# First input block of a gated state-space/GELU kernel: two 128-column pieces loaded apart, and the second one's transposes moved between matmuls

## The chip, the cores and the metric

The kernel runs on one core of a Trainium2 chip. The metric is the device time of one execution in microseconds. It is given as the median over several executions; 9 were timed for the kernel before. One further execution was recorded by the hardware profiler, and all profile numbers come from that one.

## The reference, cut to what matters

`x` has 2048 rows (time steps) of D = 640 numbers in bf16. A gate mixes a diagonal state-space layer with a dense GELU layer:

```python
g = sigmoid((x * gate_w).sum(-1, keepdims=True))
# a: h_t = Lam_bar * h_{t-1} + x_t @ B_bar^T   (complex diagonal recurrence, P = 640)
#    a = 2 * Re(h @ C^T) + x * Dskip
# b: gelu(x @ w1 + b1) @ w2 + b2               (F = 1728)
out = g * a + (1 - g) * b
```

The change concerns only the very first part of this: the product of the first 512 rows of `x` with the first 1024 columns of `w1`.

## The kernel before, in words

The 2048 rows are taken in four blocks of 512 (`q` = 0 to 3). TensorE (PE) contracts over partitions, so it needs `x` transposed: `xT[q]` holds, for each of five groups `k` of 128 input columns, a 128 x 512 tile. Most of the `xT` tiles come from transposing DMAs. Two of them, `k` = 0 and 1 of the first block, are made differently: `x` is loaded as it lies into `xn[0]` (the load `xna`, L370, 512 rows of 256 numbers, 256 KB), PE transposes it in 128 x 128 pieces against an identity matrix (L422 to L433, `xt0` to `xt3`, two pieces each, into PSUM banks 7, 6, 5 and 4), and VectorE (DVE) copies each pair from PSUM into `xT[0]` as bf16 (L436, `xc0` to `xc3`).

Before these transposes stands `warm` (L413): seven matmuls of a constant, whose result is not used. After them comes `m1_first` (L634): the first eight of the 128-column groups `jf` of `w1`, one PSUM bank (0 to 7) each, with `k` in the outer loop, so that the 40 matmuls need the tiles of `w1` and `xT[0]` one `k` after the other. Below, (k, jf) names one of them. For `k` = 0 and `jf` = 0 and 1 they are cut in halves of 256 columns, so that the first needs only `xc0`. Bank 7 serves first a transpose, then `cols` (L449: the transpose of the packed small vectors `rows`, which gives the biases and the recurrence's constants), and only then (0, 7) and (1, 7).

All further work (rest of the first product L665, `B` projection L708, second product L932, `C` projection L981, the last block's output L795 and L844) follows on PE in an order that does not change. DVE does the recurrence (L748) and the elementwise work, ScalarE (ACT) GELU and evictions.

The order is made by a small list scheduler (`Sched.order`, L43). Each operation names the keys that it reads and writes, an engine, an estimated duration and a priority; the scheduler runs an estimate of time and, on each engine, takes the released operation of lowest priority number. The result is a fixed instruction order per engine; waits are semaphores that `Emitter.wait` (L116) sets where a key was made on another engine. A DMA is an operation of the queue that issues it: `sp` (SyncE's queue, most loads, one after the other), `pool` (GpSimd's queue), and in the changed kernel also `act`. The head of SP's queue before is: `xna`; `w1` for `k` = 0; `w1` for `k` = 1; transposing load of `xT` for `k` = 2; `w1` for 2; `xT` for 3; `w1` for 3 in two parts; `xT` for 4; `w1` for 4; and then the rest of `w1`, the `B` matrices and everything else. The five loads into `rows` (L390 to L394) are on POOL's queue; the last of them is `b1b`.

Of the kernel before, what the change touches and what calls it, by code (L numbers as in the profile page):

```python
# [147 lines left out]
class Prog:  # L148
# [8 lines left out]
    def op(self, name, eng, dur, reads, writes, fn, prio=None, lat=0.0, after=()):  # L157
        deps = {}
        for k in reads:
            for w in self.last_w.get(k, ()):  # L160
                deps[w.idx] = w
        for k in writes:
            for w in self.last_w.get(k, ()):
                deps[w.idx] = w
            for r in self.last_r.get(k, ()):
                deps[r.idx] = r
        for a in after:
            deps[a.idx] = a
        deps = list(deps.values())
        E = self.E  # L170

        def run(eg, deps=deps, eng=eng, fn=fn):
            E.wait(eng, *[d.done for d in deps if not (eng == "pe" and d.eng == "pe")])
            return fn()

        it = self.sch.add(name, eng, dur, deps, run, prio=prio, lat=lat)
        for k in writes:
            self.last_w[k] = [it]
            self.last_r[k] = []
        for k in reads:  # L180
            self.last_r.setdefault(k, []).append(it)
        return it


def bass_gated_mix__ssm_conv_s5__dense_activation_gelu__prompt_kernel(
# [18 lines left out]
    _, S, D = A_x.shape  # L204
    P = A_Lambda_re.shape[0]
    F = B_w1.shape[1]
# [8 lines left out]
    FL = F - (NF - 1) * 128  # L215
# [6 lines left out]
    x2 = A_x[0]  # L222
# [3 lines left out]
    with ExitStack() as es:  # L226

        def SB(name, shape, dt):
            return es.enter_context(nc.sbuf_tensor(name, list(shape), dt))

        xT = [SB(f"xT_{i}", [128, KD, 512], BF16) for i in range(NQ)]
        xn = [SB(f"xn_{i}", [128, 4, D], BF16) for i in range(2)]
# [9 lines left out]
        rows = SB("rows", [128, 128], BF16)  # L242
# [11 lines left out]
        ident = SB("ident", [128, 128], BF16)  # L254
# [40 lines left out]
        PS = [es.enter_context(nc.psum_tensor(f"ps{i}", [128, 512], FP32)) for i in range(8)]  # L295
# [13 lines left out]
        op = pr.op  # L309

        def inc(eng, ins):
            return E.inc(eng, ins, eng + "_s")

        def dma_inc(eng, ins, sem):
            SEM(sem)
            E.count.setdefault(sem, 0)
            ins.then_inc(sems[sem], 16)
            E.count[sem] += 16
            return (sem, E.count[sem])

        def d_act(n):
            return 0.26 + n * 0.00084
# [4 lines left out]
        def d_mm(n):  # L327
            return n / 2400.0 + 0.004


        def load(name, eng, sem, dst, src, writes, prio, dur=0.5, lat=2.5, reads=(), after=()):
            def fn():
                with nc.allow_non_contiguous_dma(reason="columns of small vectors"):
                    return dma_inc(eng, engines[eng].dma_start(dst, src), sem)
            return op(name, eng, dur, reads, writes, fn, prio=prio, lat=lat, after=after)
# [16 lines left out]
        nmain = (NF - 1) * 128  # L352
# [7 lines left out]
        def w1load(k, eng, prio):  # L360
            edges = [0] + ([WSPLIT[k] * 128] if k in WSPLIT else []) + [FW]
            for i, (f0, f1) in enumerate(zip(edges, edges[1:])):
                load(f"w1_{k}{i}", eng, f"l_w1{k}{i}", W1sb[:, k, f0:f1], B_w1[k * 128:(k + 1) * 128, f0:f1], [("w1", k, i)], prio=prio + 0.1 * i, lat=2.6)

        def w1tok(k, jf):
            return ("w1", k, int(jf >= WSPLIT.get(k, NW)))

        KN = 2

        load("xna", "sp", "l_xna", xn[0][:, :, 0:KN * 128], x2[0:512, 0:KN * 128].rearrange("(c p) d -> p c d", p=128), ["xna"], 0, dur=0.45, lat=2.0)  # L370
        w1load(0, "sp", 1)
        w1load(1, "sp", 1.3)
        xtrans(0, range(KN, KN + 1), 1.6, 0.8)
# [10 lines left out]
        RT = 3 * KP + NF - 1  # L384
# [5 lines left out]
        for i, (nm, (r0, src)) in enumerate(ROWS.items()):  # L390
            src = src.rearrange("(k p) -> k p", p=128)
            load(nm, "pool", "l_" + nm, rows[r0:r0 + src.shape[0], :], src, [nm], prio=-50 + i, dur=0.6)
        load("b1b", "pool", "l_b1b", rows[RT:RT + 1, :].rearrange("o (a p) -> o a p", a=2),
             B_b1[nmain:F].rearrange("(o p) -> o p", o=1).unsqueeze(1).broadcast_to([1, 2, FL]), ["b1b"], prio=-45, dur=0.6)  # L394

        def f_iota():
            inc("pool", nc.gpsimd.iota(io_i[:, :], pattern=[[1, 128]], base=0, channel_multiplier=-1))
# [13 lines left out]
        one = nc.const_aps.tensor(1.0, [128, 1], BF16)  # L411

        def f_warm():  # L413
            t = None
            for n in (512,) * 6 + (256,):
                t = nc.tensor.matmul(PS[4][:, 0:n], one.broadcast_to([128, 128]), one.broadcast_to([128, n]), start=True, stop=True)
            return inc("pe", t)

        op("tload", "act", 1.5, (), ["tl"], lambda: inc("act", nc.scalar.activation(tl[:, :], one, ACT.Exp)), prio=-1000)
        op("warm", "pe", 2.7, (), [("bank", 4)], f_warm, prio=-1000)  # L420

        for i, (k, c0, c1) in enumerate(((0, 0, 2), (0, 2, 4), (1, 0, 2), (1, 2, 4))):  # L422
            bank = (7, 6, 5, 4)[i]
            pt = PS[bank][:, 0:(c1 - c0) * 128]

            def f_xt(k=k, pt=pt, c0=c0, c1=c1):
                t = None
                for c in range(c0, c1):
                    t = nc.tensor.matmul(pt[:, (c - c0) * 128:(c - c0 + 1) * 128], xn[0][:, c, k * 128:(k + 1) * 128], ident[:, :],  # L429
                                         start=(c == c0), stop=(c == c1 - 1), skip_group_check=True)  # L430
                return inc("pe", t)

            op(f"xt{i}", "pe", 0.11 * (c1 - c0), ["xna", "ident"], [("bank", bank)], f_xt, prio=-990 + i)  # L433

            def f_xc(k=k, pt=pt, c0=c0, c1=c1):
                return inc("dve", nc.vector.tensor_copy(out=xT[0][:, k, c0 * 128:c1 * 128], in_=pt))  # L436

            op(f"xc{i}", "dve", 0.42, [("bank", bank)], [("xT", 0, k, c0)], f_xc, prio=-2000 + i)

        XK0 = [[("xT", 0, k)] for k in range(KD)]  # L440
        XK0[0] = [("xT", 0, 0, 0), ("xT", 0, 0, 2)]
# [141 lines left out]
        for ci, src in enumerate((A_B_re, A_B_im)):  # L583
            for i, (p0, p1) in enumerate(((0, 512), (512, KP * 128))):
# [1 line left out]
        xtrans(1, range(KD), 32, 3.4)  # L586
        load("gwb", "sp", "l_gwb", gwb[:, :], gate_w.partition_broadcast(128), ["gwb"], prio=32.2)
        load("xnb", "sp", "l_xnb", xn[0][:, :, KN * 128:D], x2[0:512, KN * 128:D].rearrange("(c p) d -> p c d", p=128),
             [("xn", 0, 0), ("xn", 0, 1)], 32.4, dur=1.0, lat=6.0, reads=["xna"])
        big = load("w2a", "sp", "l_w2a", W2sb[:, 0:NF - 1, :], B_w2[0:nmain, :].rearrange("(j p) d -> p j d", p=128), ["w2a"], prio=33, lat=8.0)  # L590
        load("w2b", "sp", "l_w2b", W2sb[0:FL, NF - 1, :], B_w2[nmain:F, :], ["w2b"], prio=34, lat=4.0)
        load("w2c", "sp", "l_w2c", W2sb[64:64 + FL, NF - 1, :], B_w2[nmain:F, :], ["w2c"], prio=34.2, lat=4.0)
# [12 lines left out]
        def pe_prio():  # L605
            ctr["pe"] += 1
            return ctr["pe"]
# [26 lines left out]
        def m1_first():  # L634
            seq = [(k, jf) for k in range(KD) for jf in range(NW)]
            seq.remove((0, NW - 1))
            seq.insert(seq.index((1, NW - 1)), (0, NW - 1))
            steps = [(0, 0, 0), (0, 1, 0), (0, 0, 1), (0, 1, 1)] + [(k, jf, None) for k, jf in seq if k or jf > 1]
            for k, jf, h in steps:
                t0, t1 = (0, 512) if h is None else (256 * h, 256 * h + 256)  # L640

                def f_mm(jf=jf, k=k, t0=t0, t1=t1):
                    return inc("pe", nc.tensor.matmul(PS[jf][:, t0:t1], W1sb[:, k, jf * 128:(jf + 1) * 128], xT[0][:, k, t0:t1],  # L643
                                                      start=(k == 0 and t0 == 0), stop=(k == KD - 1), skip_group_check=jf < 2))

                op(f"m1_0_{jf}_{k}_{t0}", "pe", d_mm(t1 - t0), (XK0[k] if h is None else XK0[k][h:h + 1]) + [w1tok(k, jf)], [("bank", jf)],
                   f_mm, prio=pe_prio())
            for jf in range(NW):
                ctr["bank"] += 1

                def f_ge(jf=jf):
                    return inc("act", nc.scalar.activation(Gl[0][:, jf, :], PS[jf][:, :], ACT.Gelu_apprx_tanh, bias=b1col[:, jf:jf + 1]))

                op(f"ge_0_{jf}", "act", d_act(512), [("bank", jf), "b1col"], [("gl", 0, jf)], f_ge, prio=10)
# [269 lines left out]
        def outsT(q, mid=None):  # L924
# [85 lines left out]
            op(f"sto{q}", "sp", 0.5, [("xn", q % 2, 0), ("xn", q % 2, 1)], [], f_st, prio=403 + q, lat=3.0)  # L1010

        m1_first()
        m1(0, NW)
        bproj(0)
# [82 lines left out]
```

## Time and profile before

| | |
|---|---|
| median of 9 executions | 213.07 us (212.77 to 213.62) |
| the profiled execution's own time | 213.65 us |
| its span in the profile | 212.3 us |
| PE busy in the span | 208.5 us (98%) |
| DVE busy | 190.5 us (90%) |
| ACT busy | 103.2 us (49%) |
| chain of work that ended last | PE 97%, DMA 1% |
| `xna` issued / landed | 0.74 / 3.74 us |
| first PE transpose / first matmul of `m1_first` | 3.79 / 4.71 us |

The span is counted from the first instruction to the last. The busy share of PE is modelled from pipelined matmuls, so it does not say that PE runs at its peak; the distance between the starts of successive matmuls does. Most groups of lines stand at the line of the operation itself, but elementwise DVE work made through the helper `tt` stands at L499 and all plain loads at L334.

### The profile page before, as it was taken

The page shows a single profiled execution, that of the slowest core. Times are in us where ns is not written, and L with a number is a line of the kernel's source. Part 1 is how long each engine was busy: PE and PEld are TensorE (multiplying, and loading weights), DVE is VectorE, ACT ScalarE, POOL GpSimd, SP SyncE. Part 2 cuts the span into 40 slices and gives each one's busy share as a digit, 9 for nine tenths or more (in the row PEclk, how much of TensorE's full clock was granted, in tenths as well). Part 3 has the DMA queues.
Part 4 walks back from the last instruction along what each step waited for, and adds up shares of the span by engine and source line. Part 5 has one row for each costly group of instructions (what it writes and reads, how often), then busy time and mean ns, then how long its engine had stood idle before and what let it go on. Part 6 is the DMA issues. An engine that isn't in the chain of part 4 may idle for free.

```text
span 212.3 us, 2737 instructions
## 1 busy us (share of the span) xinstructions
PE 208.5 (98%) x1088; PEld 104.9 (49%) x1102; DVE 190.5 (90%) x240; ACT 103.2 (49%) x178; POOL 6.9 (3%) x17
## 2 busy tenths in 40 slices
PE   8999999999999999999999999999999999999996
PEld 3444444444464444444464444444446444567775
DVE  2299999999999999999999999899999999499744
ACT  2199556667960253556681063455660027623330
POOL 6000000030000000000000000000010000000000
DMA  6998999999800020056274000002853000005251
GB/s 165 228 275 168 147 131 220 317 260 197 191 14 3 0 49 0 0 50 149 52 56 117 3 0 0 0 2 66 110 124 124 0 3 0 0 0 102 69 141 62
DMA packets 48763, 19.07 MB, mean 90 GB/s; under 512 B 41584, under 2 KB 47600, under 8 KB 48752
## 3 DMA queue, kind: packets, MB, share of 16 engines
q1 hardware_dynamic: 46992, 17.59, 39.9%
q0 software_dynamic: 1760, 1.32, 4.8%
q8 instruction: 8, 0.13, 0.4%
q14 instruction: 3, 0.02, 0.1%
HBM read 8.41 MB, written 2.63 MB: 52 GB/s over the span
## 4 chain that ended last, share of the span: by engine, by line
PE 97%; DMA 1%; issue 0%; DVE 0%
PE ps L665 22%; PE ps L708 20%; PE ps L932 20%; PE ps L981 15%; PE ps L795 7%; PE ps L844 5%; PE ps L643 4%; DMA xn<-in_A_x_dram 1%; PE ps L686 1%; PE ps L943 1%; PE ps L429 0%; PE ps L809 0%; DVE W1sb L878 0%; DVE cols L454 0%; PE ps L449 0%
## 5 line engine op out<-in xcount | busy, mean ns | idle before, releaser
L665 PE MATMUL ps<-xT,W1sb 128*128 128x512 bf16 x215 | 47.5, 379 | 0.3
L748 DVE TENSOR_TENSOR_SCAN W<-atab,V 128x1280 bf16<-128x1280 f32 x16 | 44.3, 2811 | 0.3
L708 PE MATMUL ps<-xT,BT 128*128 128x512 bf16 x196 | 43.1, 379 | 0.3 <-issue 0.2
L932 PE MATMUL ps<-Gl,W2sb 128*128 128x512 bf16 (+1 forms) x230 | 42.5, 343 | 0.2
L672 ACT ACTIVATE Gl<-ps,cols 128x512 bf16<-128x512 f32 x44 | 29.9, 695 | 15.5 <-PE ps L665 15.5
L665 PEld LDWEIGHTS ps<-xT,W1sb 128*128 128x128 bf16 x220 | 21.6, 98 | 25.9
L981 PE MATMUL ps<-Hb,CT 128*128 128x512 bf16 x150 | 32.9, 379 | 0.0
L932 PEld LDWEIGHTS ps<-Gl,W2sb 128*128 128x128 bf16 x234 | 22.9, 98 | 19.3
L708 PEld LDWEIGHTS ps<-xT,BT 128*128 128x128 bf16 x200 | 19.5, 98 | 23.7 <-ACT Gt L694 0.4
L717 ACT ACTIVATE U<-ps 128x512 bf16<-128x512 f32 x40 | 23.6, 599 | 14.3 <-PE ps L708 14.3
L950 ACT ACTIVATE E1T<-ps,cols 128x512 bf16<-128x512 f32 (+1 forms) x18 | 9.5, 624 | 36.0 <-PE ps L943 36.0
L981 PEld LDWEIGHTS ps<-Hb,CT 128*128 128x128 bf16 x150 | 14.5, 98 | 17.9 <-issue 0.6
L989 ACT ACTIVATE E2T<-ps 128x512 bf16<-128x512 f32 x15 | 9.1, 604 | 13.6 <-PE ps L981 13.6
L795 PE MATMUL ps<-W2sb,Gl 128*128 128x320 bf16 x104 | 14.8, 299 | 0.0
L618 DVE SCALAR_TENSOR_TENSOR trf<-xn,gwb 128x640 bf16<-128x640 bf16 x16 | 13.2, 823 | 0.4
L499 DVE TENSOR_TENSOR V<-V,W 128x1280 bf16<-128x1280 bf16 x16 | 12.5, 822 | 0.3
L499 DVE TENSOR_TENSOR Hb<-Hb,V 128x1280 bf16<-128x1280 bf16 x16 | 12.5, 822 | 0.3
L499 DVE TENSOR_TENSOR V<-mr,U 128x2560 bf16<-128x2560 bf16 x8 | 11.9, 1492 | 0.3
L795 PEld LDWEIGHTS ps<-W2sb,Gl 128*128 128x128 bf16 x104 | 10.1, 98 | 4.3 <-issue 0.3
L499 DVE TENSOR_TENSOR Hb<-c,W 128x2560 bf16<-128x2560 bf16 x8 | 11.9, 1490 | 0.2
L499 DVE TENSOR_TENSOR V<-s,W 128x2560 bf16<-128x2560 bf16 x8 | 11.9, 1484 | 0.0
L499 DVE TENSOR_TENSOR W<-mi,U 128x2560 bf16<-128x2560 bf16 x8 | 11.9, 1484 | 0.0
(96 smaller groups left out, 154.9 us busy)
## 6 DMA issues: line engine op xcount, KB each, us to landing
W2sb<-in_B_w_dram SPq DMA_DIRECT2D x1, 2080.0 KB, 9.1
out_dram<-xn SPq DMA_DIRECT2D x3, 640.0 KB, 4.8
xn<-in_A_x_dram POOLq DMA_DIRECT2D x2, 640.0 KB, 7.2
W1sb<-in_B_w_dram SPq DMA_DIRECT2D x4, 256.0 KB, 3.9
trf<-grow SPq DMA_DIRECT2D x3, 256.0 KB, 5.3
xn<-in_A_x_dram SPq DMA_DIRECT2D x1, 640.0 KB, 7.3
W1sb<-in_B_w_dram SPq DMA_DIRECT2D x1, 480.0 KB, 4.4
out_dram<-W1sb SPq DMA_DIRECT2D x3, 160.0 KB, 1.8
```

The costliest lines, as they stand in the source:

```text
L499: return inc("dve", nc.vector.tensor_tensor(out=o, in0=a, in1=b, op=o_))
L618: t = inc("dve", nc.vector.scalar_tensor_tensor(out=scr[:, :], in0=xn[q % 2][:, c, :], scalar=1.0, in1=gwb[:, :], op0=ALU.mult, op1=ALU.mu ...
L665: t = nc.tensor.matmul(PS[bank][:, :], W1sb[:, k, jf * 128:(jf + 1) * 128], xT[q][:, k, :], start=(k == 0), stop=(k == KD - 1))
L672: return inc("act", nc.scalar.activation(Gl[q % 2][:, jf, :], PS[bank][:, :], ACT.Gelu_apprx_tanh, bias=b1col[:, jf:jf + 1]))
L708: t = nc.tensor.matmul(PS[bank][:, :], BT[:, ci, kd, k * 128:(k + 1) * 128], xT[q][:, kd, :], start=(kd == 0), stop=(kd == KD - 1))
L717: return inc("act", nc.scalar.activation(dst, src, ACT.Copy, scale=1.0 if ci == 0 else -1.0))
L748: t = inc("dve", nc.vector.tensor_tensor_scan(out=g[:, ci, :], data0=a, data1=v[:, ci, :], initial=0.0, op0=ALU.mult, op1=ALU.add))
L795: t = nc.tensor.matmul(PS[bank][:, 0:HALF], Gl[q % 2][:, jf, t4 * 128:(t4 + 1) * 128], W2sb[:, jf, cols], start=False, stop=False, skip_gr ...
L844: t = nc.tensor.matmul(PS[bank][:, 0:n], H[b % NHB][:, ci, k, s * 128:(s + 1) * 128], CT[:, ci, k, cols], start=(i == 0), stop=(i == 2 * K ...
L932: t = nc.tensor.matmul(PS[bank][:, 0:t1 - t0], W2sb[:, jf, d * 128:(d + 1) * 128], Gl[q % 2][:, jf, t0:t1], start=(jf == 0), stop=False)
L950: return inc("act", nc.scalar.activation(E1T[:, d, t0:t1], PS[bank][:, 0:t1 - t0], ACT.Identity, bias=cols2[:, 0, d:d + 1]))
L981: t = nc.tensor.matmul(PS[bank][:, :].rearrange("p (s t) -> p s t", s=2), CT[:, ci, k, d * 128:(d + 1) * 128], Hb[:, 2 * (q % 2):2 * (q % ...
```

## The change

- `xna` becomes two loads, `xna0` (columns 0 to 127) and `xna1` (columns 128 to 255), 128 KB each, rows of 256 bytes instead of 512. On SP's queue `xna1` stands after the load of `w1` for `k` = 0, so that the queue's head is `xna0`, `w1` 0, `xna1`, `w1` 1, and then as before.
- The transposes for `k` = 0 stay ahead of `m1_first`. The four for `k` = 1 become one operation into bank 6, which waits for `xna1` and follows the matmul (0, 2). Two DVE copies of 256 columns follow it, as before.
- `warm` has five matmuls of 512 columns and one of 128, instead of six of 512 and one of 256. A matmul `fill` of 256 columns of the constant stands after the transposes for `k` = 0.
- The load `b1b` is issued from ACT's queue, after ACT's first table load and its small activation, instead of as the fifth load of POOL's queue.
- The scheduler places `cols` earlier: before, it stood after (2, 0); now it stands after (1, 4), and (0, 7) and (1, 7) come before (2, 0) instead of after (2, 1).

The order on PE from the start, built from the two kernels:

```
before: warm x7 | 8 transposes | (0,0) (0,1) halves | (0,2)..(0,6) | (1,0)..(1,6) | (2,0) | cols | (2,1) | (0,7) (1,7) | (2,2)...
after:  warm x6 | 4 transposes | fill | (0,0) (0,1) halves | (0,2) | 4 transposes | (0,3)..(0,6) | (1,0)..(1,4) | cols | (1,5) (1,6) | (0,7) (1,7) | (2,0)...
```

(Before, banks 5 and 4 are taken in that order after bank 3, that is (0, 5) ahead of (0, 4).)

```diff
-        load("xna", "sp", "l_xna", xn[0][:, :, 0:KN * 128], x2[0:512, 0:KN * 128].rearrange("(c p) d -> p c d", p=128), ["xna"], 0, dur=0.45, lat=2.0)
+        for k in range(KN):
+            load(f"xna{k}", "sp", f"l_xna{k}", xn[0][:, :, k * 128:(k + 1) * 128], x2[0:512, k * 128:(k + 1) * 128].rearrange("(c p) d -> p c d", p=128),
+                 [f"xna{k}"], 1.2 * k, dur=0.45, lat=2.0)
...
-        load("b1b", "pool", "l_b1b", rows[RT:RT + 1, :].rearrange("o (a p) -> o a p", a=2),
-             B_b1[nmain:F].rearrange("(o p) -> o p", o=1).unsqueeze(1).broadcast_to([1, 2, FL]), ["b1b"], prio=-45, dur=0.6)
+        load("b1b", "act", "l_b1b", rows[RT:RT + 1, :].rearrange("o (a p) -> o a p", a=2),
+             B_b1[nmain:F].rearrange("(o p) -> o p", o=1).unsqueeze(1).broadcast_to([1, 2, FL]), ["b1b"], prio=-101, dur=1.2)
...
-            for n in (512,) * 6 + (256,):
+            for n in (512,) * 5 + (128,):
...
-        for i, (k, c0, c1) in enumerate(((0, 0, 2), (0, 2, 4), (1, 0, 2), (1, 2, 4))):
-            bank = (7, 6, 5, 4)[i]
+        def xtp(k, c0, c1, bank, prio, after=()):
             pt = PS[bank][:, 0:(c1 - c0) * 128]
...
-            op(f"xt{i}", "pe", 0.11 * (c1 - c0), ["xna", "ident"], [("bank", bank)], f_xt, prio=-990 + i)
...
+            op(f"xt{k}{c0}", "pe", 0.11 * (c1 - c0), [f"xna{k}", "ident"], [("bank", bank)], f_xt, prio=prio, after=after)
+            for h in range(c0, c1, 2):
+
+                def f_xc(h=h):
+                    return inc("dve", nc.vector.tensor_copy(out=xT[0][:, k, h * 128:(h + 2) * 128], in_=pt[:, (h - c0) * 128:(h - c0 + 2) * 128]))
+
+                op(f"xc{k}{h}", "dve", 0.35, [("bank", bank)], [("xT", 0, k, h)], f_xc, prio=-2000 + 4 * k + h)
+
+        xtp(0, 0, 2, 7, -990)
+        xtp(0, 2, 4, 6, -989)
+
+        def f_fill():
+            return inc("pe", nc.tensor.matmul(PS[4][:, 0:256], one.broadcast_to([128, 128]), one.broadcast_to([128, 256]), start=True, stop=True))
+
+        op("fill", "pe", 0.1, (), [("bank", 4)], f_fill, prio=-980)
...
-                op(f"m1_0_{jf}_{k}_{t0}", "pe", d_mm(t1 - t0), (XK0[k] if h is None else XK0[k][h:h + 1]) + [w1tok(k, jf)], [("bank", jf)],
+                mm = op(f"m1_0_{jf}_{k}_{t0}", "pe", d_mm(t1 - t0), (XK0[k] if h is None else XK0[k][h:h + 1]) + [w1tok(k, jf)], [("bank", jf)],
                    f_mm, prio=pe_prio())
+                if (k, jf) == (0, 2):
+                    xtp(1, 0, 4, 6, pe_prio(), [mm])
```

More of the change, by code (lines that the diff above doesn't have):

```diff
@@ L420, in bass_gated_mix__ssm_conv_s5__dense_activation_gelu__prompt_kernel, with f_xt @@
         op("warm", "pe", 2.7, (), [("bank", 4)], f_warm, prio=-1000)
-        for i, (k, c0, c1) in enumerate(((0, 0, 2), (0, 2, 4), (1, 0, 2), (1, 2, 4))):
-            bank = (7, 6, 5, 4)[i]
+        def xtp(k, c0, c1, bank, prio, after=()):
             pt = PS[bank][:, 0:(c1 - c0) * 128]
-            def f_xt(k=k, pt=pt, c0=c0, c1=c1):
+            def f_xt():
                 t = None
@@ L431, in f_xt @@
                 return inc("pe", t)
-            op(f"xt{i}", "pe", 0.11 * (c1 - c0), ["xna", "ident"], [("bank", bank)], f_xt, prio=-990 + i)
-            def f_xc(k=k, pt=pt, c0=c0, c1=c1):
-                return inc("dve", nc.vector.tensor_copy(out=xT[0][:, k, c0 * 128:c1 * 128], in_=pt))
-            op(f"xc{i}", "dve", 0.42, [("bank", bank)], [("xT", 0, k, c0)], f_xc, prio=-2000 + i)
+            op(f"xt{k}{c0}", "pe", 0.11 * (c1 - c0), [f"xna{k}", "ident"], [("bank", bank)], f_xt, prio=prio, after=after)
[8 more added lines that the diff above has]
+        op("fill", "pe", 0.1, (), [("bank", 4)], f_fill, prio=-980)
         XK0 = [[("xT", 0, k)] for k in range(KD)]
@@ L588, in bass_gated_mix__ssm_conv_s5__dense_activation_gelu__prompt_kernel @@
         load("xnb", "sp", "l_xnb", xn[0][:, :, KN * 128:D], x2[0:512, KN * 128:D].rearrange("(c p) d -> p c d", p=128),
-             [("xn", 0, 0), ("xn", 0, 1)], 32.4, dur=1.0, lat=6.0, reads=["xna"])
+             [("xn", 0, 0), ("xn", 0, 1)], 32.4, dur=1.0, lat=6.0, reads=["xna0", "xna1"])
         big = load("w2a", "sp", "l_w2a", W2sb[:, 0:NF - 1, :], B_w2[0:nmain, :].rearrange("(j p) d -> p j d", p=128), ["w2a"], prio=33, lat=8.0)
```

## The prediction

> **What bounds the kernel now.** I read the chain that ended last first, in order of time. Columns: start, length, what.
>
> ```profile
> 0.74 3.00 DMA xn<-in_A_x_dram
> ...
> 3.79 1.03 PE ps L429 x8
> 4.83 4.15 PE ps L643 x17
> 8.98 0.07 PE ps L449
> ...
> 9.07 0.20 DVE cols L454
> ...
> 9.32 3.41 PE ps L643 x15
> ```
>
> A load for the first 3.74 us, then PE; after 9.32 the chain stays on PE until 210.32 us, with no wait that I can find between matmuls. PE's order after `m1_first` does not change, so a shift of PE by some amount at (2, 2), which starts at 9.76, shifts the end by as much. Only the first 10 us have to be costed. There I read the waits (us in total, times, longest):
>
> ```profile
> PEld ps L429 <- DMA xn<-in_A_x_dram: 0.8, 1, 0.8
> PEld ps L643 <- DVE xT L436: 0.5, 2, 0.3
> PEld ps L643 <- DVE cols L454: 0.4, 1, 0.4
> ```
>
> These are waits of weight loads, which run ahead of the matmuls. PE's own gaps, from the starts in the trace, are 3.50 to 3.79 (`xna`), 4.62 to 4.71 (first DVE copy), and 9.09 to 9.32, where (0, 7) waits for DVE to empty `cols` from bank 7. Next, PE's timeline, 3 to 6 us and 6 to 9 us (start, length, row):
>
> ```profile
> 2.44 1.27 PE L416 MATMUL ps<-const-bfloat16-1.0 128*128 128x512 bf16 x3
> 3.79 1.03 PE L429 MATMUL ps<-ident,xn 128*128 128x128 bf16 x8
> 4.71 1.89 PE L643 MATMUL ps<-xT,W1sb 128*128 128x256 bf16 x6
> ...
> 5.53 3.45 PE L643 MATMUL ps<-xT,W1sb 128*128 128x512 bf16 x13
> ```
>
> Start to start, 512 columns take 427 ns up to 6.39, the next 270 ns, all later ones 216 ns. PE thus goes to full rate at about 6.50 (0.27 = c + (0.427 - c)/2 gives c = 0.11 after 6.39). Work placed before that costs double, and time gained there is worth half. Last, when loads land after issue (the rows are `xna`, `w1` for k = 0, k = 1, k = 2):
>
> ```profile
> xn<-in_A_x_dram SPq DMA_DIRECT2D x1, 256.0 KB, 3.0
> W1sb<-in_B_w_dram SPq DMA_DIRECT2D x1, 256.0 KB, 3.1
> W1sb<-in_B_w_dram SPq DMA_DIRECT2D x1, 256.0 KB, 4.2
> W1sb<-in_B_w_dram SPq DMA_DIRECT2D x1, 256.0 KB, 4.3
> ```
>
> Issued at 0.74, 1.26, 1.80 and 3.52, they land at 3.74, 4.38, 6.01 and 7.84; first needed at 3.79, 4.71, 7.09 ((1, 0)) and 8.60 ((2, 0)). Later loads have more slack: `w1` for k = 3 lands at 8.79 and (3, 0) starts at 11.06.
>
> **What the Trainium skill says.** "TensorE: Matmul & The Clock Gate", part 1, says that PE starts at half clock and goes to full clock after one busy window of about 3.4 us, and that the windows run freely, so that the moment varies between executions. The trace agrees on the factor (427 against 216 ns); the switch came 5.7 us after the first matmul. "DMA: Bandwidth & Descriptors", "Queues, rings and completion order": each DMA engine takes one queue's descriptors in order. The trace agrees: the 2 KB packets of `w1` 0 begin when `xna`'s 512-byte packets (1.87 to 3.08) run out. Same page, "Specifications": below 512 B per row the line rate is lost. The trace has 27 ns for a 512 B packet and 18 ns for the 256 B packets of the transposing loads: half the bytes for two thirds of the time.
>
> **The change part by part**, against the profiled execution.
>
> *`xna0`.* Still 512 packets, half the size. Packets start 1.13 us after issue, and the first 0.6 us bring only some 130 at any size. If count sets the rest, nothing is gained; if packet time does, a third of the other 0.6 us, 0.2; if bytes set all of the 1.21 us, 0.6. I take 0.25: landing 3.50, first transpose 3.54. Range 3.19 to 3.79.
>
> *Transposes, `fill`, first matmul.* From the first transpose to (0, 0) is 0.92 us (3.79 to 4.71), set by two transposes, a DVE copy of 0.43 and its semaphore, not by PE; the eight transposes (8 x 0.107 = 0.85) nearly filled it. Now four (0.43) and `fill` (256 columns, 0.21) fill 0.64 and PE idles 0.28. `fill` itself costs nothing, being under that wait. (0, 0) starts at 3.54 + 0.92 = 4.46: 0.25 earlier. `w1` 0 must be there: it is still second on the queue and now stands behind half the bytes, so it lands at 4.38 at the latest, and it does not decide. With (0, 0) at 4.46 it has little to spare; were `xna0` 0.35 earlier still, `w1` 0 could take that over.
>
> *The moved transposes.* Four at half rate between (0, 2) and (0, 3): 4 x 0.107 = 0.43 us, now uncovered. `xna1` is issued at 1.80 (where `w1` 1 was) and streams after `w1` 0, whose packets end near 3.7: some 0.8 us of packets, then 0.6 from last packet to landing as for `xna`, so about 5.1. It is needed at 4.46 + 0.82 + 0.43 = 5.71. Bounds 4.7 to 6.0, the latter being `w1` 1's old landing in the same slot.
>
> *A new wait at (0, 6).* It reuses bank 6, so both copies must be done. In the trace, from the start of a pair's last transpose to the weight load freed by the second copy is 1.16 us (3.87 to 5.03). Transposes 5.71 to 6.14, the last starts at 6.03, so (0, 6) can start at 7.19. PE does (0, 3), (0, 4), (0, 5) at 6.14, 6.54, 6.75 and is ready at 6.97: 0.22 lost.
>
> *`cols` earlier.* (1, 0) 7.41, (1, 4) 8.27, `cols` 8.49; the small loads landed at 7.64 at the latest before. From `cols` to (0, 7) was 0.50 (8.82 to 9.32). Now (1, 5) and (1, 6) lie in between (2 x 0.216): (0, 7) at 8.99. The 0.23 gap is gone but for 0.02. DVE's constants start 0.3 earlier; that shortens nothing, as PE does not wait for them.
>
> *Queues.* SP issues one load more ahead of `w1` 1: it and all after it are issued 0.52 later. `w1` 1 lands at about 6.5 (needed 7.41), `w1` 2 at about 8.35; (0, 7) and (1, 7) now come first, so (2, 0) needs it only at 9.42. If all later landings slip by 0.5, the next tightest is `w1` 4 (11.23, needed 12.8). So this is hidden by PE's own work. `b1b` saves POOL an issue of 0.52 with nothing behind it until 45 us, and costs ACT an issue while it idles until 9.3; landing together with the others, it changes nothing.
>
> *Sum.* (1, 7) 9.21, (2, 0) 9.42, (2, 1) 9.64, (2, 2) 9.86 against 9.76: 0.1 us later. As terms: start -0.25, `cols` gap -0.21, transposes +0.43, wait at (0, 6) +0.22, and -0.09 because part of the extra work displaces half-rate work. If PE changed rate at 5.0, `w1` 2 would have held the old kernel at (2, 0), and the same working gives -0.07; at 7.6 the wait at (0, 6) disappears and it gives -0.15. Since the moment may vary, I take -0.05 over executions. The profiled execution took 213.65, 1.35 above its span and 0.58 above the median of 213.07; I apply the change to the median: 213.0.
>
> **Rivals.**
>
> *A, a wash (the forecast), 55%.* Terms within their bounds: -0.35 to +0.4, so 212.7 to 213.5.
>
> *B, slower by a late clock, 17%.* PE idled 0.38 us between `warm` and (0, 0) before; now `warm` ends at 2.97, and the gaps are 0.57 + 0.28 = 0.85. If a window with that much idle does not count as busy, full rate comes one window later: 3.4 us at half rate cost 1.7, so up to 214.7, or about 213.6 to 214.2 if it hits part of the executions. For it: from 0.75 to 3.09 PE was busy in some two thirds of a window and it did not switch one window before 6.50. Against: three quarters is more than that. It decides when the share needed lies above 75%.
>
> *C, slower by a late `xna1`, 12%.* At 6.05 instead of 5.1 the transposes wait 0.34 and everything behind them follows: +0.43, 213.5. For it: the slot's old user landed at 6.01, sharing with POOL's small loads and a transposing load. Against: the load that shared with it now stands later.
>
> *D, faster by an early `xna0`, 16%.* Bytes set the stream: landing 3.15, first transpose 3.19, start gain 0.60 instead of 0.25, half or all of which counts depending on the clock: -0.1 to -0.4, and 212.5 with a late clock. For it: 128 KB is half. Against: the packet count is the same and the first packets come slowly.
>
> **How the numbers follow.** Within 0.2% is 0.43 us, about what a measurement of this kernel can tell from no change. B and C are slower (29%), D counts as faster (16%), A is the same. The likeliest time is A's, 213.0. The range goes below A for half of D, to 212.5, and above it through C and the lower part of B, to 214.0; about a tenth is left out on either side. A's own range is 212.7 to 213.5.
>
> **What would show each step.** After: `xna0` landing near 3.50 and the first transpose with it; (0, 0) 0.92 after that; L430 in two groups, the second near 5.7 without a wait for a DMA (right for A; a wait there is C); a wait of a matmul for the DVE copy of about 0.2 before (0, 6); no gap after `cols`; starts going from 427 to 216 ns near 6.5 (near 9.9 is B); no wait for `w1` 1 or 2. The prediction is wrong if the rate changes more than a window away from where it did, if 256-byte rows stream much slower than 18 ns a packet, or if PE waits for a later load.

## The result, and the profile after

The changed kernel took 215.12 us (median of 17 executions, 213.52 to 215.84). The kernel before, timed beside it, took 213.17 us (median of 52, 212.77 to 214.05). The ratio is 1.0073, 95% interval 1.0060 to 1.0086: slower by 1.3 to 1.8 us, and above the predicted range. (The means differ by 1.55 us, the medians by 1.95, because the executions of after lie in two groups; here and below I go by the ratio and its interval.) These executions are also spread in a way that those of before are not. Five of the 17 lie under 214.0 and the other twelve between 214.31 and 215.84, while none of the 52 of before is above 214.05.

The profiled execution took 214.8 us with a span of 213.2 us, 0.9 more than before. First the chain of work that ended last, in order of time (start, length, what):

```profile
0.74 0.47 SPq L334
...
1.27 3.66 DMA W1sb<-in_B_w_dram
4.93 0.14 issue
5.06 1.44 PE ps L653 x5
6.50 0.43 PE ps L430 x4
6.93 2.56 PE ps L653 x9
9.48 0.06 PE ps L459
9.54 3.48 PE ps L653 x16
```

The load at its head is no longer `xna` but `w1` 0 (`W1sb`), which lands at 4.93. Behind `cols` (L459) no DVE piece stands any more. Next, PE's waits in the first 12 us (us in total, times, longest):

```profile
PE ps L653 <- DMA W1sb<-in_B_w_dram: 1.1, 1, 1.1
...
```

One wait for the weights of the first matmul, where before there was none. PE's timeline, 3 to 5.2 us and 5.2 to 8 us:

```profile
2.44 0.74 PE L418 MATMUL ps<-const-bfloat16-1.0 128*128 128x512 bf16 x2
3.15 0.61 PE L430 MATMUL ps<-ident,xn 128*128 128x128 bf16 x4
3.54 0.42 PE L446 MATMUL ps<-const-bfloat16-1.0 128*128 128x256 bf16 x1
5.06 0.37 PE L653 MATMUL ps<-xT,W1sb 128*128 128x256 bf16 x1 [1.10 <-DMA W1sb<-in_B_w_dram]
...
6.29 0.63 PE L430 MATMUL ps<-ident,xn 128*128 128x128 bf16 x4
```

`fill` starts at 3.54 and has 0.21 us of work at half rate, so it is done at 3.76 (the row's length is the modelled end of a pipelined matmul). PE then stands until 5.06: 1.30 us. With the 0.17 between `warm` and the transposes it idles 1.47 us, where before it was 0.38. The landings after issue (the rows are `w1` 0, `xna0`, `xna1`, `w1` 1):

```profile
W1sb<-in_B_w_dram SPq DMA_DIRECT2D x1, 256.0 KB, 3.7
xn<-in_A_x_dram SPq DMA_DIRECT2D x1, 128.0 KB, 2.4
xn<-in_A_x_dram SPq DMA_DIRECT2D x1, 128.0 KB, 3.6
W1sb<-in_B_w_dram SPq DMA_DIRECT2D x1, 256.0 KB, 4.0
```

`w1` 0 took 3.7 us where it had taken 3.1, although it now stood behind half the bytes.

The matmuls around 8 us, from four narrow windows of the timeline:

```profile
7.15 1.04 PE L653 MATMUL ps<-xT,W1sb 128*128 128x512 bf16 x2
8.00 0.40 PE L653 MATMUL ps<-xT,W1sb 128*128 128x512 bf16 x1
8.24 0.38 PE L653 MATMUL ps<-xT,W1sb 128*128 128x512 bf16 x1
8.45 0.38 PE L653 MATMUL ps<-xT,W1sb 128*128 128x512 bf16 x1
```

The starts of the matmuls go from 427 to 216 ns apart, with 236 ns between 8.00 and 8.24, so the rate changes at about 8.05 us; before it was 6.50. From (2, 7) on, both kernels have the same work, and it starts at 11.78 instead of 10.84. That is +0.94, the whole difference of the spans. It can be split. Let one us at half rate count as 0.5 of work. Then from (0, 0) to (2, 7) before did 1.79 us at half rate, 4.34 at full rate and lost 0.23 behind `cols`: 0.90 + 4.11 = 5.01 of work. After does 2.99 at half rate and 3.73 at full rate: 1.50 + 3.73 = 5.23, which is more by the four moved transposes. So:

| | us |
|---|---|
| (0, 0) later: 5.06 against 4.71 | +0.35 |
| four transposes, at full rate | +0.21 |
| gap behind `cols` gone | -0.23 |
| full rate reached later after (0, 0): 1.20 us more at half rate | +0.60 |
| sum | +0.93 |

The largest term, the later full rate, is one that the forecast put at nothing and left to rival B.

### The profile page after: what moved, and what is told of

It is laid out like the page before. It is cut to its first block, busy times and chain, and to the rows that moved or that the text cites. A ratio compares the mean times of both kernels' runs of the same rounds, so it can differ in the third digit from the quotient of the medians.

```text
span 213.2 us, 2739 instructions
## 1 busy us (share of the span) xinstructions
PE 208.5 (98%) x1088; PEld 104.8 (49%) x1102; DVE 190.7 (89%) x240; ACT 103.5 (49%) x178; POOL 6.3 (3%) x16
## 4 chain that ended last, share of the span: by engine, by line
PE 96%; DMA 2%; issue 1%; SPq 0%; DVE 0%
PE ps L677 22%; PE ps L720 20%; PE ps L944 20%; PE ps L993 15%; PE ps L807 7%; PE ps L856 5%; PE ps L653 5%; DMA W1sb<-in_B_w_dram 2%; PE ps L698 1%; PE ps L955 1%; PE ps L821 0%; SPq L334 0%; PE ps L430 0%; DVE W1sb L890 0%; PE ps L459 0%
```

## The experiments

I set two theories against each other. **The clock**: PE goes to full rate at the end of a stretch of time, a window, in which it was busy enough. The gap of more than a microsecond makes the window that contains it fail, so full rate comes a window later in most executions; this is rival B, with the gap made larger by `w1` 0. **The path**: what costs is the later (0, 0), the transposes and the wait at (0, 6), and the clock would have come as it did. "TensorE: Matmul & The Clock Gate", part 1, in the Trainium skill gives the window as about 3.4 us and free-running. No run here measures its length; I use 3.41 to count the idle time of PE in the stretch that ended where the rate changed.

The letters in the expectations below are not those of the prediction. There, theory C is the clock, with its windows of 3.41 us from that page, and rival L is the path. Theory B says that the packets of `b1b` on ACT's queue hold up `w1` 0, and rival X that something else does. Theory D says that `w1` 0 lands late for a reason in the kernel, and rival H that it was chance in one execution. Rival G says that the loss grows evenly with idle time.

### The same kernel again

No edit.

> The changed kernel unchanged, for a second profile and as the base of the other runs. In its first profile xna0 landed at 3.10, w1 for k = 0 at 4.93, PE idled 1.3 us from 3.76 to 5.06, and matmuls went to full rate near 8.1. Theory D (the weight load lands late for a reason that lies in the kernel): w1 0 lands between 4.6 and 5.3 again. Rival H (a hiccup of that one execution): it lands at 4.0 to 4.4. Theory C (the idle stretch delays the full rate of PE): whatever the landing, the time follows the moment of the full rate, about 0.5 us of time per us of that moment. Median 215.1 +- 0.4 for all.

Measured: 214.35 (213.36 to 215.76, 9 executions) beside 213.41, ratio 1.0048 (1.0021 to 1.0075). The median is below the 214.7 to 215.5 that I expected. Four of the nine lie below 214.0, five above 214.3. The profiled execution, of 213.36 us, belongs to the lower group: its `w1` 0 landed at 4.62, (0, 0) started at 4.76, and the rate changed within the gap before it, between 3.69 and 4.76. Its span is 211.9 us, less than the 212.3 of before. So one program makes both times, and the head of the kernel tells them apart: in every profile of this case the span is the start of (2, 7) plus 201.4 us, within 0.1. Here (0, 6) waited 0.37 us for the second DVE copy, because PE was already at full rate; in the first profile, at half rate until 8.05, it did not wait.

### The gap filled, all else as in the changed kernel

```diff
-    return inc("pe", nc.tensor.matmul(PS[4][:, 0:256], ...))   # fill
+    for n in (512,) * 3:
+        t = nc.tensor.matmul(PS[4][:, 0:n], ...)
```

> Changed kernel, fill made of three matmuls of 512 columns instead of one of 256 (fill is no part of the computation). It ends at about 3.54 + 1.28 = 4.82 instead of 3.76, so it stands under the wait for w1 0 and PE idles some 0.2 to 0.4 us instead of 1.3 before the first product. Theory C: PE counts as busy, full rate comes at 4.2 to 7.6 as in the kernel before and the median falls by 0.8 to 1.6 us, to 213.5 to 214.3, with a spread like that of before. Rival L (the loss is the late landing and the uncovered transposes themselves; the moment of the full rate doesn't depend on idling): the median stays at 215.1 +- 0.3.

Measured: 213.95 (213.46 to 214.64, 22) beside 213.41, ratio 1.0024 (1.0014 to 1.0035). PE's timeline:

```profile
3.10 0.61 PE L430 MATMUL ps<-ident,xn 128*128 128x128 bf16 x4
3.50 1.05 PE L448 MATMUL ps<-const-bfloat16-1.0 128*128 128x512 bf16 x3
5.00 0.38 PE L656 MATMUL ps<-xT,W1sb 128*128 128x256 bf16 x2 [0.45 <-DMA W1sb<-in_B_w_dram]
```

(0, 0) starts at 5.00, hardly earlier than the 5.06 of the changed kernel, and `w1` 0 is as late, at 4.87. More useless work on PE nevertheless brought the time down, from +0.48% (the repeat, on the same chip) or +0.73% to +0.24%. The intervals of the repeat and of this run overlap; what decides is the spread: 15 of the 26 executions of the changed kernel are above 214.7, and none of the 22 here. The rate changed at 3.98 in this profile. The path alone can't do that; the clock can. The 0.24% that remain, 0.3 to 0.75 us, are what is left for the path, if the clock is then as in the kernel before.

### A gap put into the kernel before

```diff
-            for n in (512,) * 6 + (256,):   # warm
+            for n in (512,) * 5 + (128,):
```

> Kernel before, with only its warm-up shortened as in the change (five matmuls of 512 and one of 128 columns; no part of the computation). Loads and all else as before. PE idles 0.82 us instead of 0.29 ahead of the first transpose. Theory C: part of the executions reach the full rate later, the median rises by 0.3 to 1.2 us and the slowest execution by more than 1 us. Rival L: the median stays at 213.15 +- 0.15, since nothing waits for the warm-up.

Measured: 214.33 (213.00 to 215.65, 22) beside 213.41, ratio 1.0038 (1.0021 to 1.0055). Loads and (0, 0) are as before (4.42 and 4.73). PE's timeline, 3 to 7 us, of an execution of 215.65 us:

```profile
2.44 0.74 PE L416 MATMUL ps<-const-bfloat16-1.0 128*128 128x512 bf16 x2
3.81 1.03 PE L429 MATMUL ps<-ident,xn 128*128 128x128 bf16 x8 [0.64 <-DMA xn<-in_A_x_dram]
5.13 2.34 PE L643 MATMUL ps<-xT,W1sb 128*128 128x256 bf16 x6
```

The only new thing is that PE stands from 2.97 to 3.81, 0.84 us, ahead of the transposes, which does not delay them. The rate changed at 9.46, (2, 7) started at 12.32 and the span was 213.7: 1.4 longer than before, from a gap that nothing waits for. That execution was the slowest of the 22; over all of them the loss is 0.8 us (0.4 to 1.2). Twelve of the 22 executions are above 214.25, none of the 54 of before.

### How much idle time a window takes

```diff
-            for n in (512,) * 6 + (256,):   # warm
+            for n in (512,) * 5 + (384,):
```

> Kernel before with a warm-up of five matmuls of 512 and one of 384 columns (no part of the computation): it ends at 3.18, PE idles 0.61 us ahead of the first transpose and 0.09 before the first product, against 0.29 and 0.09 before and 0.84 and 0.09 in the run with the shorter warm-up (214.33, up to 215.65). Theory C with a threshold of some 0.85 us of idling in a window: 0.70 stays below it, so full rate comes little later than before: median 213.4 to 213.7, nothing above 214.6. Rival G (the loss grows evenly with idling): halfway, median 213.8 to 213.95, some executions above 215.

Measured: 213.57 (212.96 to 214.51, 14) beside 213.55, ratio 1.0001 (0.9986 to 1.0017); two of the 14 above 214.25. Here PE idled some 0.8 us in the stretch that counted. The other end is no warm-up at all:

```diff
-            for n in (512,) * 6 + (256,):   # warm
+            for n in (128,):
```

> Kernel before with the warm-up cut to one matmul of 128 columns (no part of the computation). PE idles until 3.79. Theory C: the first window that counts as busy must hold less than 0.85 us of idling, so it ends no earlier than 3.79 + 3.41 - 0.85 + 0.09 = 6.4 and no later than 9.9: full rate at 6.4 to 9.9, every execution slow by 0.5 us per us against an early one: median 1.2 to 1.8 above before, lowest execution at 213.7 or more, highest near 215.8. Rival L: nothing waits for the warm-up, 213.4.

Measured: 214.57 (213.69 to 215.49, 12) beside 213.44, ratio 1.0056 (1.0038 to 1.0073). That is about 1.2 us by the ratio and 1.1 by the medians, at the lower end of what I expected or just under it. The rate changed at 9.07.

In eight profiles, PE's idle time in the 3.41 us that ended where the rate changed, and in the stretch one window earlier where it did not (time before the first instruction is counted as idle):

| kernel | rate changed at | idle in that window | idle one window earlier |
|---|---|---|---|
| before | 6.50 | 0.37 | 1.11 |
| changed | 8.05 | 0.43 | 1.06 |
| three `fill` matmuls | 3.98 | 0.34 | |
| moved transposes alone | 5.45 | 0.65 | |
| `b1b` back on POOL | 3.58 | 0.76 | |
| `warm` 5 x 512 + 384 | 5.54 | 0.83 | 2.06 |
| `warm` 5 x 512 + 128 | 9.46 | 0.00 | 0.93 |
| `warm` 128 | 9.07 | 0.00 | 1.67 |

Five more profiles fit: the windows that counted hold 0.1 to 0.7 us of idle time there. In the repeat the moment is not exact enough. No window with 0.83 us or less failed and none with 0.93 or more counted. So the limit would lie between, at a busy share of 73 to 76% of 3.41 us. It rests on one profile on each side and on the assumed length, and one spread fits it badly: with `b1b` back on POOL (next section) PE idled over 0.9 us between `warm` and (0, 0) in the profile, as much as in the kernel with the gap put in, yet only one of 14 executions is above 214.4. Either (0, 0) came earlier in the others or the limit is less sharp than it looks; the runs do not tell which. With 1.47 us of idle time between 2.97 and 5.06, a window of the changed kernel counts only if it ends by about 4.4 or begins after about 4.2. As the windows begin at any moment, that leaves a change of rate at about 3.5 to 4.4 in 0.9 of 3.41 cases (26%) and at 7.8 to 10.3 in the others. This is an estimate worked out from the limit, the assumed length of the window and the first profile. Of the 26 executions of the changed kernel, 9 are below 214.0 (35%).

### `b1b` back on POOL's queue

```diff
-        load("b1b", "act", ..., prio=-101, dur=1.2)
+        load("b1b", "pool", ..., prio=-45, dur=0.6)
```

> Changed kernel with b1b back on POOL's queue. In the first profile the packets of b1b ran at 2.25 to 2.75, just before the packets of w1 0 stood for 0.4 to 0.9 us each. Theory B (the second hardware queue disturbs the weight load): w1 0 lands at 4.0 to 4.5 and the median falls by 0.5 us or more. Rival X (it is the order of SP's own queue, or the switch to 2 KB packets): it lands at 4.7 to 5.2 again and the median stays at 215.1 +- 0.4.

Measured: 214.02 (213.06 to 215.54, 14) beside 213.41, ratio 1.0016 (0.9998 to 1.0035), which is not clearly different from before. The landing of `w1` 0, issued at 1.27, in this kernel:

```profile
W1sb<-in_B_w_dram SPq DMA_DIRECT2D x1, 256.0 KB, 3.1
```

It landed at 4.39 instead of 4.93, and (0, 0) started at 4.53. With the four packets of `b1b` gone from the first microseconds, a 256 KB load on another queue came 0.2 to 0.5 us earlier than in the three profiles that have them there. What this variant gave up is the early `cols`, and so the 0.23 us behind it are back (the chain has a DVE piece for `cols` at 8.21).

The same with a longer `fill`:

```diff
+ the edit above, and fill with
+            for n in (512,) * 2:
```

> Changed kernel with both suspects taken out: b1b on POOL's queue as before, and fill of two matmuls of 512 columns (no part of the computation), so that PE is busy to about 4.35. Theory C (clock by free windows of 3.41 us, of which PE may idle no more than some 0.85 us): no window idles so much, full rate comes at 3.4 to 7.0 as in the kernel before, w1 0 lands near 4.4 and the first product starts near 4.5. Left over: the wait at (0, 6), up to 0.37 at full rate, and the transposes, against the earlier start and the gap after cols. Median 213.2 to 213.7 where before has 213.4, spread under 1.5 us. Rival L (the moved transposes and the split load are the loss): 214.0 or more, as b1b on POOL alone gave 214.0.

Measured: 213.92 (213.12 to 214.53, 22) beside 213.55, ratio 1.0014 (1.0003 to 1.0026). This did not win, and came out above the 213.2 to 213.7 that I expected, although `w1` 0 landed at 4.19 and (0, 0) started at 4.38, 0.33 earlier than before. What stood against it shows on PE: `cols` waited 0.14 for `b1b`, which landed at 7.82 as POOL's last small load, (0, 7) lost 0.23 behind `cols`, and (0, 6) waited for the second copy.

### The moved transposes alone

```diff
-        for k in range(KN):
-            load(f"xna{k}", ..., [f"xna{k}"], 1.2 * k, ...)
+        load("xna", ..., ["xna0", "xna1"], 0, ...)
...
-            for n in (512,) * 5 + (128,):   # warm
+            for n in (512,) * 6 + (256,):
```

`b1b` is on POOL's queue as before.

> Changed kernel with the load of both blocks in one as before, the warm-up as before, and b1b on POOL's queue: only the transposes of the second block are moved, with fill, and cols stands earlier. First transpose at 3.79, first product at 4.71. By the prediction's terms: +0.43 for the transposes at half rate or +0.22 at full rate, +0.2 to +0.4 for the wait at (0, 6), -0.2 for the gap after cols: 0.2 to 0.5 above before. If the move itself did most of the harm: 1 us or more above before.

Measured: 213.98 (213.33 to 214.75, 22) beside 213.55, ratio 1.0026 (1.0015 to 1.0037), or 0.3 to 0.8 us. The chain between 4.77 and 8.66:

```profile
4.77 1.13 PE ps L651 x5
5.90 0.24 PE ps L428 x4
...
6.16 0.77 DVE xT L436 x2
...
6.97 1.68 PE ps L651 x7
```

The DVE copies of the moved transposes stand on the chain: (0, 6) starts 0.581 after (0, 5) where 0.216 would do, so the wait is 0.37. The transposes and their wait cost by themselves 0.21 to 0.43 and 0.37, and only an earlier start can pay for that.

### `b1b` late on ACT's queue, a longer `fill`

```diff
-             ..., ["b1b"], prio=-101, dur=1.2)
+             ..., ["b1b"], prio=-101, dur=1.2, reads=["xna0"])
...
+            for n in (512,) * 2:   # fill
```

This keeps all of the change, and takes away both suspected causes: `b1b` is issued only after `xna0` has landed (at 3.16), and `fill` covers the gap.

> Changed kernel with fill of two matmuls of 512 columns (no part of the computation) and b1b still on ACT's queue, but issued only when xna0 has landed (about 3.1). Theory B (the packets of b1b on the second hardware queue, at 2.3 to 2.75, hold up the first packets of w1 0): w1 0 lands at 4.1 to 4.5, as in the two runs with b1b on POOL's queue (4.39 and 4.19). Rival X (it landed at 4.62 to 4.93 in the three runs with b1b on ACT's queue for another reason, the two others being chance): 4.6 to 5.0 here too. With either, the clock theory expects a median of 213.5 to 214.0 and no execution above 214.7, since PE idles under 0.85 us.

Measured: 213.34 (213.10 to 213.92, 14) beside 213.44, ratio 0.9996 (0.9984 to 1.0007): no difference from before that can be measured, and less than the 213.5 to 214.0 that I expected. The landing of `w1` 0, and then the chain:

```profile
W1sb<-in_B_w_dram SPq DMA_DIRECT2D x1, 256.0 KB, 3.0
```

```profile
0.78 2.40 PE ps L418 x6
...
3.18 0.61 PE ps L430 x4
3.79 0.85 PE ps L448 x2
4.65 1.28 PE ps L656 x5
5.93 0.40 PE ps L430 x4
...
6.36 0.77 DVE xT L438 x2
```

`w1` 0 landed at 4.25 and (0, 0) started at 4.44. No load stands in this chain; by the starts, PE idles only 0.21 us ahead of the transposes. The rate changed at 6.16, near the 6.50 of the kernel before. Counted as above, the terms are: start -0.27, transposes +0.21, gap behind `cols` -0.23, wait at (0, 6) +0.37, half rate from (0, 0) on -0.04. That makes +0.04; (2, 7) started at 10.93 against 10.84, +0.09, and the span was 212.4 against 212.3. The prediction had +0.1. Start and gap agree with it one by one. The other two errors cancel: the wait was 0.37 instead of 0.22, and the transposes with the half-rate work that they displace cost 0.17 instead of 0.43 - 0.09 = 0.34.

### The early `cols` without the rest

First `b1b` alone on ACT's queue, in the kernel before:

```diff
-        load("b1b", "pool", ..., prio=-45, dur=0.6)
+        load("b1b", "act", ..., prio=-101, dur=1.2)
```

> Kernel before with only b1b issued from ACT's queue, which also makes the order place cols after (1, 5) instead of (2, 0). By the prediction's term the 0.23 us gap before (0, 7) goes: 0.1 to 0.25 below before. Theory B (the second hardware queue delays the weight load by 0.2 to 0.5 us): w1 0 lands at 4.6 to 4.9 instead of 4.38, the first product waits for it, and the gain is lost: 0.0 to 0.4 above before.

Measured: 213.21 (212.84 to 213.84, 22) beside 213.55, ratio 0.9995 (0.9984 to 1.0005): no clear difference. The scheduler put `cols` after (1, 5), so that one matmul alone stood between it and (0, 7), and the gap of 0.23 stayed. `w1` 0 landed at 4.40, as before: in this order `b1b`'s packets go at 2.96 to 3.18. Then with `cols` one matmul earlier still:

```diff
-        op("cols", "pe", 0.3, ..., f_cols, prio=15.5)
+        op("cols", "pe", 0.3, ..., f_cols, prio=13.5)
```

> Kernel before with b1b issued from ACT's queue and the priority of cols lowered so that it stands after (1, 4), with (1, 5) and (1, 6) between it and (0, 7), as in the changed kernel. Loads of x, transposes and warm-up as before. The 0.23 us gap before (0, 7) goes: median 0.15 to 0.3 below before if the small loads for cols have landed when PE reaches it (7.3 at an early full rate; b1a landed at 6.8 to 7.0), and 0.0 to 0.1 below if PE waits for them instead.

Measured: 212.99 (212.61 to 213.78, 22) beside 213.44, ratio 0.9982 (0.9971 to 0.9994), faster than the kernel before by 0.1 to 0.6 us, and so than both kernels. The chain:

```profile
4.70 2.88 PE ps L643 x14
7.59 0.06 PE ps L449
7.64 4.13 PE ps L643 x19
```

No DVE piece follows `cols`, where the kernel before had 0.20 of it plus its semaphores. The gap of 0.23 is down to 0.02. Finally the same with a longer `warm`:

```diff
-            for n in (512,) * 6 + (256,):   # warm
+            for n in (512,) * 7:
```

> The same with a warm-up of seven matmuls of 512 columns (no part of the computation), ending at 3.72, so that PE idles 0.07 us instead of 0.29 ahead of the first transpose. Theory C with the threshold: full rate comes 0.25 us earlier on average, at most 0.1 us of time; nothing else changes. 0.0 to 0.15 below the run without it.

Measured: 213.12 (212.64 to 213.69, 22) beside 213.44, ratio 0.9980 (0.9970 to 0.9990). Nothing more is gained: at 0.38 us of idle time the windows of the kernel before already count.

## Why the prediction was wrong

The forecast of 213.0 came from A, and B came true, with a larger gap than B had.

- **`xna0`: the term was mis-sized, on a wrong premise.** It landed at 3.10, not at 3.50, and at 3.03 to 3.14 in every variant that has it, below the range of that step and close to D's 3.15. The premise was that "the first 0.6 us bring only some 130 at any size". By 2.47 us, 132 of the 512 packets had started before and 390 after; over all profiles it is 105 to 132 for packets of 512 bytes and 355 to 416 for those of 256. Why is open. (The stream before also ran to 3.31, not to 3.08: the prediction missed its last 37 packets.) D's gain did not follow, because of the next step.
- **Transposes, `fill`, first matmul: the step that failed.** "`w1` 0 ... lands at 4.38 at the latest, and it does not decide": it landed at 4.93, and at 4.62 and 4.87 in the two other profiles with the same loads, and it did decide. (0, 0) started at 5.06 instead of 4.46, and PE idled 1.30 us behind `fill` instead of 0.28. Of the extra 1.0 us, 0.6 is the later (0, 0) and 0.4 the earlier `xna0`, since the transposes were done sooner and nothing else was there to do. The step counted the bytes ahead of `w1` 0 and left out that its own packets could take longer, as they did (below).
- **Queues: "landing together with the others, it changes nothing".** This failed too: `b1b` is the part of the change that goes with the late `w1` 0. With its four packets out at 2.44 to 2.60, `w1` 0 landed at 4.62 to 4.93; without them there, at 4.39, 4.19 and 4.25. The rest of that step held: there was no wait for `w1` 1 or 2.
- **Rival B.** Its mechanism was right, and so was about what a missed window costs. The 0.85 us of idle time that it assumed would lie at the limit worked out above (0.83 to 0.93). The idle time was 1.47, clearly above, so a miss of the window became the rule instead of a 17% case. Its "up to 214.7" was still too low for the median of 215.12, since it started from A's early (0, 0), which did not come. The longer `fill` takes away the high executions with (0, 0) still at 5.00, and the gap put into the kernel before makes such executions with nothing delayed. Together these show the cause.
- **The moved transposes, the wait at (0, 6), `cols` earlier.** As worked out, where their conditions held. The transposes waited for no DMA (`xna1` landed at 5.36, their turn came at 6.30), so C is out. The wait was 0.37 at full rate and absent at half rate, against 0.22 expected at a change of rate in between. The gap behind `cols` went to 0.02.
- **The sum.** +0.1 at the old clock came out: the variant that has neither `b1b`'s packets in the way nor the gap came to +0.09 in its profile and to a ratio of 0.9996. That two of its terms were off by 0.15 and 0.17 in opposite directions is partly luck.

How four packets of `b1b` on ACT's queue can hold up a 256 KB load on SP's by 0.2 to 0.7 us is not settled. A packet of 2 KB usually takes 84 ns. Of the first 32, those of `w1` 0, 9 to 12 take 400 ns or more in the three profiles with `b1b`'s packets ahead of them (up to 954), 3 to 5 in the three with the split load but without those packets (up to 633), and at most one where `xna` is one load. So part of the slowness comes with the split load itself, and `w1` 0 gained at most 0.2 us from the halved bytes ahead of it: 4.19 to 4.39 without `b1b`'s packets, against 4.38 before. The traces show that these packets are slow, not what they wait for. "DMA: Bandwidth & Descriptors", "Queues, rings and completion order", in the Trainium skill has each DMA engine take turns between the queues that have work for it, one packet at a time; no run here shows why four small packets should then cost more than their turns. The cause stands on three profiles with and three without, one execution each. In the kernel before, `b1b` on ACT's queue did no harm: its packets went at 2.96 to 3.18 there and `w1` 0 landed at 4.40.

## What to carry to other kernels

While the clock still has to rise, idle PE time can cost more than it seems to: 0.84 us without matmuls, which nothing waited for, cost 0.8 us over all executions here and 1.4 in the profiled one, and cheap matmuls placed under the wait of the changed kernel took most of its loss back. When a load is made earlier, look at what is needed next and work out when that lands with everything that now leaves at the same time, small loads included. A change of several parts can carry one good part: here it was the earlier `cols`, worth 0.18% alone (0.06 to 0.29) and lost in the rest.

## What the runs showed of the hardware

- In the 3.41 us before the rate of PE rose (a length assumed above, not measured), PE idled up to 0.83 us. Stretches with 0.93 or more did not raise it. Matmuls of a constant counted as busy: they fill most of the stretch before 3.98 us in the variant with three `fill` matmuls. So did transposes by matmul: if they counted as idle, the stretch that raised the rate with `warm` 5 x 512 + 384 would have 1.66 us of idle time, more than the 1.46 of a stretch of the changed kernel that did not raise it.
- One and the same program reached full rate between 3.69 and 4.76 us in one profile and at 8.05 in another, and its executions differ by over 2 us.
- 128 KB in 256-byte packets of 18 ns landed 2.3 to 2.4 us after issue, 256 KB in 512-byte packets of 27 ns 3.0 to 3.1 us after it. In the first 0.6 us of the stream 355 to 416 of the small packets started, and 105 to 132 of the large ones.
- Four small packets on ACT's queue, at 2.4 to 2.6 us, went with a landing 0.2 to 0.7 us later of a 256 KB load that SP had issued at 1.27; at 2.96 to 3.18 us they did not.
